# Another order of all engines' steps in a fused memory attention and MLP kernel, and one add moved from GpSimd to VectorE

## The chip, the cores and the metric

The kernel runs on one core of a Trainium2 chip. The time is device time in microseconds from launch to end; three runs of the kernel before gave a median of 710.39 us (709.92 to 711.08). The profile names the core's engines PE (TensorE, matrix products; its weight loads are shown apart as PEld), DVE (VectorE), ACT (ScalarE), POOL (GpSimd) and SP (SyncE, which here only issues DMA transfers).

## The reference

x is 2048 x 512. It is normalized by rows, and the result xn goes into two branches, which meet in one product:

```
out = x + attention(xn) * silu(relu(xn @ w1) @ w2)

attention: 32 heads of 16 columns, 4 segments of 512 rows
for s in range(4):
    logits = qs @ ks.T / 4 + causal mask         # within the segment
    a_dot  = softmax(logits) @ vs
    pq     = phi(qs)                             # t + 1 for t > 0, else exp(t)
    o      = g * (pq @ M) / (pq @ z + 1e-6) + (1 - g) * a_dot     # g = sigmoid(beta), by head
    M     += phi(ks).T @ vs                      # memory, 16 x 16 for each head
    z     += phi(ks).sum(rows)
attention = o @ wo
```

w1 is 512 x 1792, w2 is 1792 x 512, and wq, wk, wv and wo are 512 x 512. All is float32.

## The kernel before

**Precision by parts.** Operands of the large products are split into a rounded part and a rest (names that end in h and l: wh and wl, xh and xl, hh and hl, oh and ol). A product is three matmuls, h x h, h x l and l x h, summed in PSUM. The split of a weight tile of 128 x 512 is one ACT copy (L409, wh) and one POOL subtraction (L410, wl) for each of 176 tiles.

**Halves of the array.** Most products run with 64 rows of the array at a time. `lanes` (L743 and L751) pairs the lower half of a chain's next product with the upper half of an earlier one, so that two streams share PE. A step of three such pairs takes about 0.68 us and is the unit of filler work: the projections to q, k and v, the two MLP products (`w1chain`, `w2chains`) and the output product of all segments but the last.

**A chain of the MLP.** `w1chain` for a block f of 128 hidden columns is four steps on one PSUM bank. Then ACT writes hh (relu, L783), and DVE writes hl (L784), which is the bank's last reader and so sets it free.

**A unit of attention** is 4 heads of one segment, 32 units in all. q and k of two units come from one projection (`projout`, L973 and L974 split it, L977 and L978 write it to DRAM, `stack` reads it back in the shape that the logits need, L1112). `rowmax` has five steps, k0 to k4, of four small matmuls each (L1138), and DVE reduces every block to row maxima (L1144, tile md; a step's bank is free when its reductions are done). `maxrows` turns the maxima (L1162) and sends them through DRAM into the rows of q (L1164, L1165), so that the five `expo` steps (L1190) give logits less their maximum; ACT takes the exponential (P), POOL zeroes above the diagonal (L1197), and `pv` (L1238) multiplies with v. `numden` reads the memory, `memory` and `memory2` add to it; DVE turns phi(k) for it in 16 small transposes (L1072).

**Constants.** `gates` makes the sigmoid of beta and lays it out for each head group: a DMA of beta, a tanh on ACT (L385), and on DVE a step of nine small instructions, here called picks (L370 to L382), which also reads blk, a mask that POOL builds (L336 to L339).

**The end.** `wlast` is the output product of the last segment: row tiles 0, 1 and 2 of 128 rows and 512 columns, and row tile 3 as two halves of 256 columns. `output` multiplies a tile with the gate branch on DVE (L884), adds the rows of x on POOL (L888, with `onpool`) or on DVE (L886) and issues the store (L890). `outhalf` does the same for the halves of tile 3 (L916, L918, L920).

**What sets the order.** Nothing is scheduled at run time. `emit` describes some 4000 steps in a first order, each for one engine: 1121 for PE, 1051 for DVE, 622 for ACT, 525 for POOL and 695 for SP. `Tape.play` then takes them from that list in the order that the string ORDER gives: each letter is the place, in what is left of the list, of the step to emit next. Each engine runs its own steps in that order, and waits where a step needs a result or a buffer of another engine. The string BANKS gives, for each use of PSUM in the first order, the bank that it gets. Both strings were found by a search outside the kernel; the kernel holds only its result. The numbers of steps below count one engine's steps from 0.

Of the kernel before, what the change touches and what calls it, by code (L numbers as in the profile page):

```python
# [77 lines left out]
ORDER = (  # L78
    "0AzByAxwCEAtAsXEqTppTUnTTTkTXiTWgWiAheSBAfSabbbgaAeCAXXN9DNXMMMALTMLLLOADJAPIiJoAHDPAFGFAFDACOpCMISGABAAAODGILeC"
    "HDbEaV1RKXDWWbWGVODFSWUVZUUUaWZCVVCVUUCeVLcXVOZTUnPSSpmkPWlAeQbAgUMWQabXRMJcaLSZUJKPV9LHKNPQMK1NSAMAIOHHIGIJJIG)"  # L80
    "aKMLHKLHIKIIAI^EKJFHJFLFIjFJKHHIHGJGLHIGGGIGIVHGULGGFOFJMFNLIIKJIJKJVLRVJFHOPLJOMKILFJHHoHFQIkG!pIpjHilL15e30GqI"
    "eJnxwkIcH=Gjal*psJentZlhpZhd-hXkYdF5dospgaZFn6kWc3X3lgadHfdeXjalaaXjZjFUdhadfEbSZSWWfXhXeERbeUaSEVRFnTWbPSjZthSP"
    "QplV2PEiOOzRQvCfWphWZanlRVkzAUVQwNwhTMCeNQoOCvaQmWlYRVoCeRTMQOQaJfCTMQMJLbNCUUCjlnQDjKjKiEnRLyJDjQJbCCOCGonLGUCD"
    "SsPDQDoaiCCMhXEWycPclMtgPNYpYNnzeX0XEbYEaVkpYpZVXDiZfUgcXbVZJCaYXSHZVWrVCUUp?JLRbUkiUUPMINcsUZJQpX2nQC0v+vxPKGUC"
    "6t3gdDJFcnCuNE6DWPCopRTPSxlxUOPXhUOOqAKSDPBKvINhNKBQOPdJNODkNiWHRHTOWRKNJOUETNMERNNKhOdMecRc3MD1aDvYYtYuYVDvUBqu"
    "lCLnolnKmuBPglhkqPyngHmBgslHdcghjmeHAbadabe$qAQDkMclDjrYiVfVDBsTTBpEqRRoXzXWxW0XAzFeLaedWArTaVnWEXLiRAQjnEbUNFAF"
    "ZDVWYbLUHaDKCDBaYTdCWbZGCXVCUXTTCBTDBAUTCJWPTPCbACBAEALKFGegDgHgehqHbiOfHgeEveLJaOWpCaIHXjAWBYIAQvdWtVfAadUUPA2S"
    "cYzdSaFgOtY5Slg4jo0malXhvhjbQffQAggUdEjcfEKgUZYcbeUdbAZsJZQIhOZVCaTCHXAfTcAbbTgUTFeEWpcbQmVaDGiTioThgASmejXiiaIf"
    "XaJdcqZpXojdniQkcUKVuFcTiSWSYmRClTGaETZR^BA,R;AAPTPIWEQTCA#RDMSALB/nCJAHpAkFEAhEvzxI)*ftv$vf@fF/}A1-q[h[4EA+}DB8"
    "5]l[41Dr$<x0cnq9u*zAtB3w1A?7hT7fz*56wTxgBDqtV2wV@wtxpTnsSmDqYnemBlhdXPUfaohaWiWYWfcemdjjPUhnbaflZxkUiPctcgTSdnot"  # L90
    "SnmrZlqZhnndAkzkkhdefcRmcbfjRW?Zc>YhOlhqAjkZfnZNcebTceAMQUysBeVASsLSALPPAIJPMITuNAdQLKA@UK#ASL><<IIrNtqlsqAPom/v"
    "Pm-Hsg7?k7B=huiBspByj5n5JAvbkIuxf5kcacmFjnzehhhjiessagqlHihHhbHeieaAHHiLfbhobkAlWKZchYVdAdXbEkOSVZUf&S^HSd^GRSbO"
    "QJIcaXa{X(ZJPFEV2TGYNHEVQCESANCIORIQLqQMADNHHbB=nLAB*/MJqjOHImfPYhdFBDqCkocZABZZAnWeMkkdKCanAWYbBQhUVWeVQYUaUWTF"
    "BTAafSZbScDcRXVVWRxRAxQRAQQqPv2BPRJrAT4NLA3mIllHKjeIhdHLAwrOuwGIrsqsu4usrZq2ALy0x3AwtwqWxtxrlCt1D6p2qy3DGooGEmwl"
    "FtrpjomnBbYjeA1Z2dgAzKBdZMakBgLOAZROkaBMSVfWFccbFScJSRWJYMkHTVGTfUIGFdGakAaZEjYRfAdeTcRvUSQAXXRKYoTUlDdAhUMfaBL9"
    "HGPGLAXeXYMeRSaPtTzTs+PPAO6DVBy2AQFvAuJMfBsIBvHHBsuGuDltrFrDjhiErAfCwfGupznf0rwfwq4udhe0Ec2egxwfiExtkafrlchBomCk"
    "+AU5Ti5BhfPSeNypgcOhheSf+emeScL5bTLxOz-wfeBdQfMNB3wJAkKIxofitoVhHHTeNHkefAihedYtUbQIVcRGWIdPaGaeZPeBFWKkLZidTZKf"
    "gSZeLXAO^4eahKOiSoONfhkQbiQbTZeTQhfXfPRTcQATZeTYAbWSZOkUXQIXWePVGTOSAPXQVAOQMRPHCNDBbMFAaEDAGGXVDTFhRGRFCPEOEYQp"
    "bpPEDSlCP-jQ9C+gJ8IRy5P*0cZNIy6XxICI5ItKHrpJx0HrQCuxPjtntGrFNueyquerFpOnZARmmkZFNlhfXKPldDddbMfaeYQSSOiQtLJAVTCR"
    "PPCXPUcVUTIYCMHeXHeFGFCTcKTCWATWUVRASFLbaENVFDBOWIDCOBPBAQCGLJKALIINKIIGWDIETDNRDIDKCKaFUYICAGJARTMIYERAPGWTANQP"  # L100
    "VOLMoNVTMHFSQJKOJFKQINAJEAIHOGPPNGgNGhMKkmLjiEDhoiegJlbdncchbklb^iiDkhmdigIZAdhHcdrmGepbmnWcjkCjiSAZ^Sf^SEYdAM{b"
    "WdaQbBTXMXZRAGUHLCQGaBSAEWFJKDCRUAHADEALFCCz0ROCJoCLILCJaFFwlJvMCGJnGCKkAIBfAAIBbWWahHkgZkZBiBFefSdaSBaaqGKWpAPn"
    "hNTjfhDVodYgZmQMZWWabdWMYVAWDbBSKTASoAonPnPSIAqiNTn7HfceA2>LKbAyyabwJ5EMYVG01w1<CyFyV-D8k0uu6Dnjj2HQ5l5Hy4nkxgun"
    "hDqioEeikNjjfkgAzUwgAevddMDqiBdnXZBAXBYfzVXXxtbWeqU#qdQ3Aewk1vfxkwXAeW-ssYaebAZbZVgOzaAdeAccfTRkhfPhfeSNhcOQaMGL"
    "hJMYeKcdaUcLZYZMTkLGKPDIFCPbtTPrQcWQQmEvISjOMqhmOICjCQJrBh^CBoZLYVXZaXIp1YoGXKSXjKUwUTuTXScaSEBXTDkTUFbOTIbbRUEM"
    "OFWQSEbLOQjTZDYCMQVBQLPCXWdXBbPMTGiRWgRKFgeBFUceFbaUaEjYBlKSBJTJPNXMbNCUHISFYSNHHUQEXVNEdUKSaMLQNEOCSQCSGOUGNORM"
    "IZUPXYSLTWRDSQ6kSCUQPCCNcfcFcGFZKpYOFlaUjFFSOEseQsqiriHoSvzHuQjxHjtgECvgMdFdDYkEEsIbgiIfaUccljPjdndemdlViiIUagHe"
    "eIMeBPLNaLdZBYLgUceFCUbZUZUfXXEceTcbNHTaBbNDOaYZQXDWPJDqJLpmJDBQESAgBABTGQBBEOJEELCDDCAARMLLANKDRLSQPNPLPANONMMK"
    "LANBGOIRAKPPHYJMZKbKXGMXRMISUkOLikQjFRMjfeTeFLbNlQZMJKEMweNuhTQIopRn3nRI1EwExOGtX1SQeGdryReptJdOBGnwnrEZForWdNDo"
    "blDFjrClVXqEIhkYhTPXCeVdczVyVCVvRDMRRANRAOOODiLMEICJaMaSPNOMBITLSTRIJQJZPHAQNOGOBEMLIQUIPAORQOQKPAJJKLLJNGQIsLRR"  # L110
    "LobQoSmNAQOcFfRAOaYN1Q0KLVvIvREBOINANnALLAjDiQhMGLGKbKmKiakENfgtELWsVaoYDGlgkrgYWJWmEmDgxDfTxbgWXdkbZnijWSyGWWwG"
    "scVrbiFZmHaWFYbVEnJVTDjSjSSXNOehVoNfXUaUVjAD$fhgTffGUHbRwSCPt7vF3Pwgq0wIOuqoAOrEA?DW=Nl-I-WIMJdWbKJk1AXyCWS6NuUR"
    "s1sTIXALX3VHKAXSxEgMlevjhIshLSfMQwMcItjafCEAcmBcwbKCmJDaRBVmEYNDmcWAjEUDTKeCPgRJDdNONJHQIfPBdPPbBiOhOYMOdNPBbBPZ"
    "REbBQBPSPCDnFMDnPjCkDJBJjCBeD8FGZuDE4XrAMicbxHAeAaBEARAFUIFAKQAKASIIMCDAIBEAMAEDAEBGAJABFFBEAGDAECACBBA")
# [53 lines left out]
def emit(tc, PE, ACT, DVE, POOL, SP, cst, ps, dr, args):  # L168
    x2, wq, wk, wv, wo, beta, w1, w2, out2 = args
    S = Tape()  # L170
# [711 lines left out]
    def output(s, t, po, pk, onpool):  # L882
        gt, gk, xr, xk, rows = GX.pop((s, t))
        dve(512, [pk, gk], [gk], lambda: DVE.scalar_tensor_tensor(gt, po, 0.5, gt, op0=OP.mult, op1=OP.mult), 23.7)  # L884
        if not onpool:
            dve(512, [gk, xk], [gk], lambda: DVE.tensor_tensor(gt, gt, xr, op=OP.add), 10.3)  # L886
        else:
            pool(512, [gk, xk], [gk], lambda: POOL.tensor_tensor(gt, gt, xr, op=OP.add), 4.5)  # L888
# [1 line left out]
        dma([gk], [f"out{s}{t}"], lambda: SP.dma_start(out2[rows, :], gt), 10.1, "put")  # L890
# [710 lines left out]
```

## Time and profile before

| | |
|---|---|
| median of 3 runs | 710.39 us (709.92 to 711.08) |
| the profiled execution | 708.85 us |
| its span, first to last instruction | 707.1 us |
| granted TensorE clock | 0.999 |
| PE busy | 691.2 us, 98% |
| DVE, ACT, POOL busy | 70%, 58%, 63% |

The profile is of one execution. A row of the timeline gives the start and the duration in us, the engine, the line of the kernel, the operation, what it writes and reads, and in brackets the idle time of the engine before it and what ended it; "x3" stands for three instructions in a row. A row of waits gives the sum, the number and the longest.

### The profile page before, as it was taken

To read this page: it belongs to the slowest core of one execution; us is meant where nothing else is said; L and a number is where in the kernel's file an instruction comes from. 1 tells how busy PE (TensorE), PEld (TensorE's weight loads), DVE (VectorE), ACT (ScalarE), POOL (GpSimd) and SP (SyncE) were. 2 spreads that over 40 slices of the span, in tenths; PEclk is the share of its full clock that TensorE was granted. 3 is DMA by queue.
4 is the path that set the end of the run, shared out by engine and by line. 5 is a ranking of instruction groups with operands and counts; after the bars stand their busy time and mean duration, and the time that the engine had idled before them with its cause. 6 is when DMAs were issued, how large, how long until landed. Compare 5 with 4: busy or idle time off the path is not lost.

```text
span 707.1 us, 18584 instructions
## 1 busy us (share of the span) xinstructions
PE 691.2 (98%) x6770; PEld 558.5 (79%) x6770; DVE 498.1 (70%) x1591; ACT 407.4 (58%) x621; POOL 447.9 (63%) x571
## 2 busy tenths in 40 slices
PE   9989999999999999999999999999999999999996
PEld 8978777787777788787888779777778878767885
DVE  4189979679968876688965778775778457566347
ACT  5444665566676674476465583756566455655641
POOL 5451775446565686676467876688466676656576
PEclk9999999999999999999999999999999999999999
DMA  6685556556666758876676567866666786944323
GB/s 200 227 274 168 171 192 202 197 153 213 191 237 203 235 163 262 249 209 183 186 224 195 168 217 243 286 197 187 204 205 198 210 280 204 278 139 157 103 60 135
DMA packets 126452, 141.46 MB, mean 200 GB/s; under 512 B 24905, under 2 KB 70217, under 8 KB 126361
## 3 DMA queue, kind: packets, MB, share of 16 engines
...
q8 instruction: 54, 0.88, 0.6%
...
q10 hardware_dynamic: 208, 0.20, 0.1%
...
## 4 chain that ended last, share of the span: by engine, by line
PE 78%; DVE 11%; POOL 3%; ACT 3%; issue 2%; DMA 1%; SPq 1%; DVEq 0%; ACTq 0%; POOLq 0%
PE ps L743 40%; PE ps L751 12%; PE ps L1238 9%; PE ps L1138 5%; PE pt L1190 5%; DVE none L1144 4%; DVE pkT L1072 3%; POOL wl L410 2%; DVE F L1034 1%; DMA nn<-F 1%; PE pt L1024 1%; ACT pq L1032 1%; PE pt L474 1%; PE ps L699 1%; PE ps L701 1%
## 5 line engine op out<-in xcount | busy, mean ns | idle before, releaser
L410 POOL TENSOR_TENSOR wl<-io,wh 128x512 fp32r<-128x512 f32 x176 | 227.6, 1303 | 116.2 <-ACT wh L409 98.4
L1144 DVE CUSTOM_DVE_ANT_0 none<-ps,causal 128x512 bf16<-128x512 f32 (+3 forms) x512 | 249.6, 488 | 61.2 <-PE ps L1138 36.8
L1207 ACT ACTIVATE P<-pt 128x1024 f32<-128x1024 f32 x128 | 131.3, 1026 | 85.8 <-PE pt L1190 65.3
L743 PE MATMUL ps<-xh,wh 64*128 64x512 f32 x352 | 140.9, 400 | 1.0 <-DVE md L1144 0.7
L751 PE MATMUL ps<-xl,wh 64*128 64x512 f32 x352 | 141.4, 402 | 0.0
L751 PE MATMUL ps<-xh,wh 64*128 64x512 f32 x352 | 136.9, 389 | 0.0
L751 PE MATMUL ps<-xh,wl 64*128 64x512 f32 x352 | 136.9, 389 | 0.0
L743 PE MATMUL ps<-xl,wh 64*128 64x512 f32 x352 | 136.7, 388 | 0.0
L743 PE MATMUL ps<-xh,wl 64*128 64x512 f32 x352 | 136.6, 388 | 0.0
L409 ACT ACTIVATE wh<-io 128x512 fp32r<-128x512 f32 x176 | 107.3, 626 | 34.7 <-PE ps L751 23.2
L1197 POOL TENSOR_SCALAR_AFFINE_SELECT P<-P 128x512 f32<-128x512 f32 x128 | 79.8, 639 | 46.7 <-ACT P L1207 33.9
L743 PE MATMUL ps<-wh,hh 64*128 64x512 f32 x224 | 92.0, 411 | 0.4 <-DVE md L1144 0.4
L751 PE MATMUL ps<-wl,hh 64*128 64x512 f32 x224 | 91.3, 408 | 0.0
L751 PE MATMUL ps<-wh,hl 64*128 64x512 f32 x224 | 87.2, 389 | 0.0
L743 PE MATMUL ps<-wl,hh 64*128 64x512 f32 x224 | 87.1, 389 | 0.0
L751 PE MATMUL ps<-wh,hh 64*128 64x512 f32 x224 | 87.0, 389 | 0.0
L743 PE MATMUL ps<-wh,hl 64*128 64x512 f32 x224 | 87.0, 388 | 0.0
L1138 PE MATMUL ps<-ks,qs 64*128 64x512 f32 (+3 forms) x512 | 78.3, 337 | 4.1 <-DVE hl L784 2.7
L1238 PE MATMUL ps<-P,vt 128*17 128x512 f32 (+3 forms) x1024 | 75.1, 434 | 0.1
L743 PEld LDWEIGHTS ps<-xh,wh 64*128 64x128 f32 x352 | 65.0, 185 | 9.6 <-issue 2.9
L743 PEld LDWEIGHTS ps<-xh,wl 64*128 64x128 f32 x352 | 64.8, 184 | 7.4
L1190 PE MATMUL pt<-qs,ks 64*128 64x384 f32 (+3 forms) x512 | 68.3, 311 | 2.2 <-DVE F L1034 1.1
(180 smaller groups left out, 1765.9 us busy)
## 6 DMA issues: line engine op xcount, KB each, us to landing
...
```

The source lines that it names most:

```text
L409: act(512, [rk], [hk], lambda: ACT.activation(h, raw, AF.Copy), 7.0 + nsplit if early else 6.0)
L410: pool(512, [rk, hk], [lk], lambda: POOL.tensor_tensor(l, raw, r32(h), op=OP.subtract), 8.5 + 1.3 * nsplit if early else 25.4)
L474: PE.matmul(pw[:, :128], ident, ident, start=True, stop=True)
L743: i = PE.matmul(m[0], m[2][0][LO], m[2][1][LO], start=m[4], stop=False)
L751: PE.matmul(h[0], h[2][0][HI], h[2][1][HI], start=False, stop=h[5] is not None)
L1072: dve(140, fk, [k], lambda a=a, b=b, i=i: DVE.transpose(pkT[a, :, b], pv[b, i // 4]), 4.0)
L1138: PE.matmul(two[a][0][:, o:o + w], qs[r, p, w - 128:w], ks[r, p, :w], start=True, stop=True)
L1144: dve(w + 40 + TTR, [pk, "causal"], [f"{dk}.{p}{a}{j}"], lambda p=p, j=j, o=o, w=w, a=a, pS=pS: DVE.tensor_tensor_reduce(none[:, :w], pS[: ...
L1190: PE.matmul(pT[:, a, o:o + w], ks[r, p, 128 * i:128 * i + 128], qs[r, p, 128 * i:], start=True, stop=True)
L1197: pool(512, ks, ks, lambda: POOL.affine_select(t, t, pattern=[[0, 4], [1, 128]], compare_op=OP.is_ge, fill=0.0, base=0, channel_multiplier ...
L1207: act(1024, tk, [both[p]], lambda: ACT.activation(P[:, 2 * p:2 * p + 2, :], pT, AF.Exp, scale=0.25), 18.5)
L1238: PE.matmul(pO[32 * b:32 * b + 17, 128 * i:], v, P[:, b, o:o + w], start=i == 0, stop=i == 3)
```

## The change

ORDER and BANKS are replaced. The list of steps, their contents and their buffers other than PSUM banks stay as they are. In `wlast` the argument `onpool` becomes true for row tile 0 alone, where it was true for tiles 0 and 2: tile 2's rows of x are now added on DVE (L886) and not on POOL (L888).

```diff
@@ -62,56 +62,57 @@
 BANKS = (
-    "0123456454253420153452353450551404120452326703670525674146721670311675236751267326733156714140675167234067034673"
...
-    "5673067052761")
+    "0123456454214325014314232155001351341125056754674331672516725675204674206734067206723236713552671467410467012674"
...
+    "4672167456734")
...
 ORDER = (
-    "0AzByAxwCEAtAsXEqTppTUnTTTkTXiTWgWiAheSBAfSabbbgaAeCAXXN9DNXMMMALTMLLLOADJAPIiJoAHDPAFGFAFDACOpCMISGABAAAODGILeC"
-    "HDbEaV1RKXDWWbWGVODFSWUVZUUUaWZCVVCVUUCeVLcXVOZTUnPSSpmkPWlAeQbAgUMWQabXRMJcaLSZUJKPV9LHKNPQMK1NSAMAIOHHIGIJJIG)"
...
-    "s1sTIXALX3VHKAXSxEgMlevjhIshLSfMQwMcItjafCEAcmBcwbKCmJDaRBVmEYNDmcWAjEUDTKeCPgRJDdNONJHQIfPBdPPbBiOhOYMOdNPBbBPZ"
-    "REbBQBPSPCDnFMDnPjCkDJBJjCBeD8FGZuDE4XrAMicbxHAeAaBEARAFUIFAKQAKASIIMCDAIBEAMAEDAEBGAJABFFBEAGDAECACBBA")
+    "0AzAyAxwFABtAsUEqVppVTnUTZkCSXhSWSeSgAiRRdAcdTbTfTWYACaOTYASTDALTQPLLEALL+AIOILEHKHIAGKBAJFbDADYDJHICJERNjGJAgDA"
+    "eBdDCbbgbFaHDYPVGHYFMEVVNNCSMYUKORCTQBPQJOOaRUYSTWMQkMQnPkLNLiJagLXaQJXaAVNcXTTQWXJJPPTPIPJP3OASNLVHNOLJrHLeKAJ)"
...
+    "AABN.jF^AFEkEJBIIBHBHGIAXCIfEBIGOQDHDBFAIIBLGAWCYQXUZWYMVEcLHBBFpNAAocNbHkLHgAGOEGKFCAYCCDZBPBACMBDAJKKNJABHAAHB"
+    "EFEBAAA")
@@ -939,7 +940,7 @@
             if t < 3:
                 yield from project(s, t, *banks[t], us, groups)
                 if groups == one:
-                    output(s, t, *banks[t], t % 2 == 0)
+                    output(s, t, *banks[t], not t)
                 yield M3, False
             else:
```

The search behind the new strings used other durations for the steps, and let a step of PE give free what it reads in parts and not only at its end; none of that is in the kernel.

Read against the list of steps, the new order differs as follows. On PE 227 of 1121 steps keep their place, and a step moves by 2.2 places on average and 21 at most; on DVE 88 of 1051 keep it (6.0 places on average, 63 at most).

*Around picks.* PE's steps 40 to 78 come in the same order in both. On DVE:

- before: hl of f0, the q split (L974), the k split (L974), phi(k) (L991), 16 transposes among which stand the parity step (L364 to L366) and hl of f1 and f2, picks, hl of f3, reductions of unit 0
- after: the parity step, the q split, picks, the k split, phi(k), hl of f0, 15 transposes among which stand hl of f1 and f2, hl of f3, reductions of unit 0; the 16th transpose comes among the later reductions

On ACT the tanh of beta (before behind the relu of f2) comes ahead of the q split, and the exponential of phi(k) (L984) directly behind its relu (before with a weight split between). On POOL blk's last step comes ahead of the weight split of f3 (before behind the splits of three later weights). PE's step 76, `rowmax` k1 of unit 0, writes in both orders one bank that hl of f3 sets free and one that the first reduction sets free.

*Attention against filler.* PE steps from a unit's last `rowmax` step to its first `expo` step, and DVE steps from that `rowmax` step to the unit's last reduction:

| unit | PE steps before | after | DVE steps before | after |
|---|---|---|---|---|
| 3 | 32 | 19 | 8 | 11 |
| 15 | 27 | 21 | 12 | 5 |
| 19 | 32 | 21 | 12 | 5 |
| 30 | 29 | 21 | 11 | 6 |

*The end.* PE's last five steps were the halves of tile 3 (five steps); now they are a last half step of tile 3 twice, and then groups 1, 2 and 3 of tile 1. The last steps of DVE, POOL and SP:

- DVE before: L884 of tiles 0, 2 and 1, L886 of tile 1, L916 of both halves, L918 of both halves
- DVE after: L884 and L886 of tile 2, L916 of the second half, L884 of tile 0, L916 of the first half, L918 of both halves, L884 and L886 of tile 1
- POOL before: L888 of tiles 0 and 2; after: L888 of tile 0
- SP before: stores of tiles 0 and 1, of the first half, of tile 2; after: of tile 2, of the first half, of tiles 0 and 1. The second half is stored from ACT's queue in both.

More of the change, by code (lines that the diff above doesn't have):

```diff
@@ L84 @@
[L84 to L93, printed above, removed]
@@ new lines @@
+    "qlf2AViSQbyRSuZtcpVc^HRDlPW^CTDixRTviRSDtfQqQSDbvRnXUYSqjVfDQTRKPbQPZDwRbLe*!DYPpXD/Tn/vOntGNkGwMii7EhLEf2DKOJJG"
+    "mdhE-FGa8GZVEgFs>GRdDkdmcHP5kqQkDY1z(YfkqYOXcZoGqlDZMmkbYlUOcgUNSbZYZFRQRWVDXdEOVQfQULJDvKT6JNOr2NUoDMHTkGzQitAQ"
+    "JtqROFZSaFjZrwSWrtQoVoFVlNOFzVsRWOTCJSMnLn!LJJNkgN-eUdoQRCRP3PIX=jX0INexNJbJQZLJOoMNmNlCkPSPCeKDE6NubL5sQ2tLCxrt"
+    "LVrsMoykUWvpMjhmLqhDjwCofthmtnfehfmiJdJsDkhePUmQSYQjc1WiEHSTvEcFRKX6QXpCW1PDm2akOT+LRRwxCRCt+SYqHA6BWFtOBTCNRNwD"
+    "RJNtCVECIBFkBP&hRBL@EMiBJOCKIQCBSCQBQPCRJBTQIBNUSKNK2QCOINyJMqPRIOCfojecOqNapRimECqBfnimBxmwh0puyloh7nh+p58F5uMb"
@@ new lines @@
+    "B5uH/CBu3-91wFzWBX6vuF4j3sxxpwDtoTBrmapqTDnnBl2shtLmWMVmBirBWihIngvfklSr3jo1j2j7SizkJhRtiAAzzjwpWtjsJ7Vlqplb32Ov"
+    "jyuxoeR8AFxbj6vw2jPVyAxgIDAEgXXeCEabKeZZBLZPYJLKYECAH#OGVCMLDFoAEpAqnMG3Czm1y{k0p)]mxkFB&u(Kt:E$!rE9[i]{/([pzp]$"
+    "+7B)@,tDA5v2AB4/&978k?$66z>@By3c>Bb2pgA52k2BU0zVqUybkApuoall7xcyaTqmdUepildtTlkrbjyeYmnug5lfpBX3i06i0lYWvkXW1lwW"
+    "dv^Ldo^JtjsV5SqAkh2jhkfrhqCejrZephccQuXjlQcpjkocAcPS6BaTSAa1OYsWANTBSMMSQnSQAKANMTALdMcLWO1OAWuKxt]vAR]1clA$y#p!"
+    "IAz5n03BxmAjkALE+rk1ood5Aidkw0kdylKJuJ2lml1cnzmaxAQjYtiqrXmkjPIihabffDZ^ojh^mgroOeinFXgkB^aZifWWAW^QnXVAMXM^bSgV"
@@ new lines @@
+    "^IXeNEQ!DaGHdDXZaQEVFWPVISYTJCEUAPsSABAP@CSHLPzMH-OnIHMHpbFCC8mqJ5Ckn3LH1HAFrwKApE7bQ6LpcTZ2CWXjjMWtBnYqfwZkYUXr"
+    "ACfoiAm&JgTg@CSC=SCdTQS+f9BRWTRC3RwSRCQBOAONsNSNkAm*86-g6JLAd4N]5{d5R3%vI#A8v4-FvG*8dFZr2kM!y+WAimG-EY6lq1rAooZ1"
+    "xwoTmIlaeIiZDWFQigUAZeVTAWcWAMZSPSBSlbAcRVRODVNAaTAPGXQfVVPcOnTYISjlSVFiHQGSPFajXBlhS^HhXT^EAffxVTcNEmZSPLAhPmJj"
+    "WMDAfhfTKefZiBRXMeNezYPMAVZbYBqD7B<P6B-O3AL/1M0L9Lyy2L!OKKzF/4PwJH1]/2)Ipy+nKA8mCtAljIV/j+i/BFi8AZs{lEgfCBhkuw#k"
+    "CKe?kCgX*BlkjajdAKgWaXUcaXdldqCYNobnbT40c2zkcTPWwXW1dLwyQUcaOTGuyQwhLPLfrrfLH3Gc1kGfGGbceRcN3TYYAFOYQNFaYOqYXBVb"
@@ new lines @@
+    "VTLdNLQJUd^+eULWobUjaJcghZAmiTeciXcggaXZXhWbTXdSaPRZUVXSTQZURSA^NkV^5VAKTAdJTSbPNQ:MOANJILQERMAGHJA=IBHAVHJVTFDE"
+    "TRSReEDOEDsM=D$X=L!D<ZNVD[Q#PP%!&7P#JRa=4?JAa<sItCJ<@Lu7=KtK4qSqK8o7oSS2Co-RyRjlwGseGCI8zi6cdg3nNfElFScjEWWaacaN"
+    "aCt4YTTKJAbdLSDYJAJPKSNlRBLFdARbFAPasRFmAWQJJkCAWRhLHbPBBEZMFBWpGEEQEBeHNDBACJYEZZCMHEUjGSGLEORFEFORECFALKRBL^TJ"
+    "FAQLNQLRgLQRLcEKMCZLQAIBIfTOTRAGFLXGTBMTwCBHQsHPNqOzOo-BwGM8MdE6BRycdeIubcCBLWhyYgWvmHWOAGcAbnaaSUbaSTYV^FeX^TSg"
+    "IVAc^Oc^OPbTKNUXCZWBSWUHARSNPQ[JOJOBXQC!LKQEREUIFsOMDEoCKCDBJpDCKEDrAppADnFsAoFEmDnGCCiiDosoCFrIqAaoBmAkYNIQyggV"
@@ L117 @@
+    "ATq/AtU+XIazZRG*AWP9VPUG8Y7AdXPW2UD9hEy6ilki2jiN-4RVL7DTOMaNM4LX2CbJpaCX0LXWxIVUZSB0SKQUwATGMRrAcxAQEumPArTJSSoD"
+    "AABN.jF^AFEkEJBIIBHBHGIAXCIfEBIGOQDHDBFAIIBLGAWCYQXUZWYMVEcLHBBFpNAAocNbHkLHgAGOEGKFCAYCCDZBPBACMBDAJKKNJABHAAHB"
+    "EFEBAAA")
 RSTEP = (((0, 3, 0),), ((0, 0, 0), (0, 2, 128)), ((0, 1, 0), (1, 1, 256)), ((1, 0, 0), (1, 2, 128)), ((1, 3, 0),))
```

48 lines of the change are left out of this document (19 added, 29 removed).

## Prediction

> **What bounds the kernel now.** I read the head of the page first, then the busy time by stretches of 20 us, then TensorE's own waits.
>
> ```profile
> span 707.1 us, 18584 instructions
> PE 691.2 (98%) x6770; PEld 558.5 (79%) x6770; DVE 498.1 (70%) x1591; ACT 407.4 (58%) x621; POOL 447.9 (63%) x571
> ...
> 20.00:40.00 20.00, 20.00 (x159) 18.75 (x159) 5.57 (x16) 11.50 (x21) 10.45 (x17) 1.00 0.73 233
> 40.00:60.00 20.00, 16.49 (x144) 14.98 (x142) 18.70 (x62) 5.08 (x9) 7.82 (x11) 1.00 0.57 180
> 60.00:80.00 20.00, 19.50 (x208) 16.82 (x206) 18.05 (x68) 12.62 (x19) 10.52 (x14) 1.00 0.74 238
> 80.00:100.00 20.00, 20.00 (x237) 14.73 (x236) 16.91 (x63) 12.29 (x18) 11.01 (x28) 1.00 0.54 177
> ...
> PE ps L1138 <- DVE hl L784: 2.7, 1, 2.7
> PE pt L474 <- POOL epst L267: 1.4, 1, 1.4
> ```
>
> In the stretch rows the numbers after the stretch's length are the busy times of PE, its weight loads, DVE, ACT and POOL, then granted clock, share of the DMA engines and GB/s. PE is busy 98% at full clock: it sets the time, and a change of order, which leaves PE's instructions as they are, can only take away PE's idle time or add to it. That idle time is 707.1 - 691.2 = 15.9 us. 1.4 lie in the opening, and about 5.9 behind the last matmul (shown below). The largest single piece left is one wait of 2.7 us for VectorE's hl, in 40 to 60 us, where DVE is busy 18.70 of 20 while it has only 5.57 of 20 in the stretch before. All other idle time of PE together is 15.9 - 1.4 - 5.9 - 2.7 = 5.9 us.
>
> **The change, first place: the gate constants on VectorE.** What stands before the waiting matmul on DVE, and on PE:
>
> ```profile
> 27.88 0.69 DVE L784 SCALAR_TENSOR_TENSOR hl<-ps,hh 128x512 fp32r<-128x512 f32 x1 [13.07 <-ACT hh L783]
> 30.60 0.69 DVE L974 TENSOR_TENSOR F<-ps,F 128x512 fp32r<-128x512 f32 x1 [2.03 <-ACT F L973]
> 33.81 0.69 DVE L974 TENSOR_TENSOR F<-ps,F 128x512 fp32r<-128x512 f32 x1 [2.52 <-ACT pk L983]
> 36.27 0.69 DVE L991 SCALAR_TENSOR_TENSOR pk<-ps,pk 128x512 f32<-128x512 f32 x1 [1.77 <-ACT pk L984]
> 37.00 2.52 DVE L1072 STREAM_TRANSPOSE pkT<-pk 32x128 f32<-32x128 f32 x8
> 40.43 0.69 DVE L784 SCALAR_TENSOR_TENSOR hl<-ps,hh 128x512 fp32r<-128x512 f32 x1
> 44.03 0.82 DVE L370 TENSOR_SCALAR bt<-bt 128x32 f32<-128x32 f32 x1
> 44.89 1.22 DVE L374 TENSOR_TENSOR mT<-bt,blk 128x32 f32<-128x32 f32 x1
> 46.14 0.18 DVE L376 TENSOR_REDUCE gcol<-mT 64x4 f32<-64x32 f32 x1
> 47.19 0.29 DVE L382 TENSOR_SCALAR gsc<-gsc,par 128x8 f32<-128x8 f32 x1
> 47.39 0.68 DVE L784 SCALAR_TENSOR_TENSOR hl<-ps,hh 128x512 fp32r<-128x512 f32 x1
> 47.99 0.68 DVE L1144 CUSTOM_DVE_ANT_0 none<-ps,causal 128x512 bf16<-128x512 f32 x1
> ...
> 44.50 0.39 PE L743 MATMUL ps<-wh,hh 64*128 64x512 f32 x1
> 44.99 0.39 PE L751 MATMUL ps<-xh,wh 64*128 64x512 f32 x1
> 48.13 0.32 PE L1138 MATMUL ps<-ks,qs 64*128 64x128 f32 x1 [2.74 <-DVE hl L784]
> 48.73 0.55 PE L1138 MATMUL ps<-ks,qs 64*128 64x128 f32 x3 [0.28 <-DVE md L1144]
> ```
>
> The picks step (L370 to L382) holds DVE from 44.03 to 47.48, 3.45 us. Behind it on DVE stands the hl of chain f3 (47.39), which frees the PSUM bank that PE's step 76 (row maximum, L1138) writes. PE has been through since 44.99 + 0.39 = 45.38 and waits 2.74 us.
>
> The new order puts picks between the two L974, where DVE waited 2.52 us for work, and hl of f0 (before at 27.88, in a free place) behind L991. So DVE's work from L991's end at 36.96 to the hl of f3 is now: hl of f0 0.69, 15 transposes at 2.52 / 8 = 0.315, or 4.73, and hl of f1 and f2, 1.38. Sum 6.80: hl of f3 starts at 43.76 in place of 47.39 and ends at 44.45, and the first reduction (L1144, 0.68) ends at 45.13. PE needs both at 45.2 to 45.4, so the wait is gone, and the next one of 0.28 with it at best. DVE comes out 47.39 - 43.76 = 3.6 us earlier, PE 2.74: **term 1 is -2.74 us**.
>
> What picks delays in its new place: it starts at 30.60 + 0.69 = 31.29 and takes 2 us (its nine instructions at the 0.18 to 0.29 of L376 and L382) to 3.45 us (as measured). So the second L974, ready at 33.81, goes at worst at 34.74, 0.93 us late. Queued behind it is the key path: the L978 write, then the stack read for step 73, which PE reached at 43.55.
>
> ```profile
> 34.52 0.32 SPq L978 DMA_DIRECT2D sdk<-F  x1
> 38.17 0.36 SPq L1112 DMA_DIRECT2D ks<-sdk  x1
> ```
>
> From the write to the read that waits for it are 3.65 us. With as much for the read itself the keys were there at 38.17 + 3.65 = 41.8 (an estimate), 1.7 us ahead of 43.55, which covers 0.93. I price this at 0; uncovered it costs 0.93. L991 isn't late: ACT's exponential in front of it has moved ahead of a weight split. Bounds of term 1: 0, if later waits take the gain, and -3.5, all idle time of that stretch (20.00 - 16.49).
>
> **Second place: the end.**
>
> ```profile
> 700.94 0.28 PE L701 MATMUL ps<-wh,ol 128*128 128x256 f32 x1
> 699.49 0.69 DVE L884 SCALAR_TENSOR_TENSOR io<-ps,io 128x512 f32<-128x512 f32 x1
> 700.21 1.50 DVE L886 TENSOR_TENSOR io<-io,bacc 128x512 f32<-128x512 f32 x1
> 701.63 0.41 DVE L916 SCALAR_TENSOR_TENSOR io<-pt,io 128x256 f32<-128x256 f32 x1
> 702.30 1.15 DVE L918 TENSOR_TENSOR io<-io,bacc 128x256 f32<-128x256 f32 x2
> 699.87 2.96 POOL L888 TENSOR_TENSOR io<-io,bacc 128x512 f32<-128x512 f32 x2
> 703.57 0.39 SPq L890 DMA_DIRECT2D out_dram<-io  x1
> ```
>
> PE ends at 701.22. Behind it DVE still has the add of tile 1, two L916 and two L918, and POOL the add of tile 2 until 702.83, whose output is issued last, at 703.57: 2.35 us after PE, and 3.53 before the end of the span. In the new order tile 1 is PE's last, tile 2 is added on DVE (an L886 more there, an L888 less on POOL) several PE steps earlier, and both halves are through before. Behind the last matmul stand only tile 1's L884 (0.69) and L886. I price L886 at 0.69, the row of L884 with the same shape, since POOL's one add left, of tile 0, needs only a PE step that is five places before the last. With three handovers of 0.03 (699.49 + 0.69 = 700.18 to 700.21) that is 0.69 + 0.69 + 0.09 = 1.47 to the issue: **term 2 is 1.47 - 2.35 = -0.88 us**. With the measured 1.50 for L886 it would be -0.07; those are the bounds. The one more issue on SP's queue behind the halves is an old one that changes places.
>
> The row says 1.50 for an add beside POOL's adds and 0.69 for a like instruction elsewhere. The Trainium skill (SBUF — State Buffer, Who interferes with whom) states that a VectorE instruction with two SBUF inputs and a GpSimd instruction that reads SBUF exclude each other, the later one blocking until the earlier ends. By that rule the first L918 would wait for POOL's add of tile 0 and push tile 1's L884 by some 0.2 us, an estimate: term 2 would be -0.7. By the row's 1.50 it is -0.07.
>
> **The rest of the order.** Most steps move by a few places on their engine (on PE by 2.2 on average, on DVE by 6). Row maxima, exponentials and memory reads of many head groups come 2 to 5 us earlier on PE, with filler put behind. No row prices this. At best it takes all the 5.9 us of other idle time; at worst I count as much in new waits, +5.9. I take 0.
>
> **Sum:** 707.1 - 2.74 - 0.88 = 703.48. The profiled execution was 708.85, 1.75 above its span, and the median 710.39 is 1.54 above that execution. So 703.48 + 1.75 + 1.54 = **706.8** for the median.
>
> **The rivals.**
>
> *The gain is taken back in the first segment.* DVE is busy 18.70, 18.05 and 16.91 of 20 from 40 to 100 us. If DVE bounds PE there, PE waits later instead, and only term 2 stays: 709.5. For it: the 18.05. Against: term 1 takes DVE work out of that stretch and not only a wait from PE (3.45 us out, hl of f0 with 0.69 in), and PE idles only 0.50 in 60 to 80.
>
> *Slower: exponentials too early for their row maxima.* One mechanism: between a unit's last row maximum step on PE and its first exponential lie reductions, a transpose on DVE and two small DMAs (L1164, L1165). Unit 19:
>
> ```profile
> 426.04 0.49 PE L1138 MATMUL ps<-ks,qs 64*128 64x512 f32 x2
> 432.85 0.39 SPq L1164 DMA_DIRECT2D mx<-mT  x1
> 436.32 0.58 SPq L1165 DMA_DIRECT2D qs<-mx  x1
> 443.73 0.48 PE L1190 MATMUL pt<-qs,ks 64*128 64x512 f32 x2
> ```
>
> The chain took 436.90 - 426.04 = 10.9 us to the end of the last issue, and the exponential came after 17.7. The new order leaves 32 - 11 = 21 PE steps where there were 32, so about 17.7 x 21 / 32 = 11.6 us at the mean of this row, and with the landing still to come (2 to 3 us, an estimate from the 3.65 above, which has the issue in it) PE would wait about 2 us there. Units 3, 15 and 30 are shortened in the same way (listed with the change), so four times 2 us makes +8, and 706.8 + 8 = 714.8. It outweighs the gain of 3.6 once the four waits exceed 0.9 us each. Against it: for units 15, 19 and 30 the new order has 5 or 6 DVE steps from the last row maximum step to the last reduction, where there were 11 or 12, so the chain is moved up too. With half the waits, 2 of the 4, it would be 710.8.
>
> *More is won.* DVE's peaks are spread better and half or more of the 5.9 us goes too: 706.8 - 4 = 702.8. For it: PE's small waits are nearly all for DVE. Against: they are under 0.5 us each.
>
> *It doesn't do what it says.* picks needs blk from POOL and the tanh from ACT; were one late, DVE would stand with the key path behind it, up to 3 us lost, 709.8. Both stand in the new order ahead of work that PE needs at about the same time (blk's last step ahead of a weight split for chain f3), so this counts little.
>
> **How the numbers follow.** Forecast 0.60; taken back, or picks late, 0.16; slower 0.14; more won 0.10. A measurement of this kernel tells about 0.2% (1.4 us) from no change. Forecast and more won are faster, 0.70; taken back is within, 0.16 with 0.01 less for its upper tail, 0.15; slower 0.15. The forecast's own range is 705.0 to 708.6 (the bounds of terms 1 and 2 mostly). The range for 8 in 10 goes from 702.5 (more won) to 711.8 (0.2% over before, with the smaller of the slower cases).
>
> **What would show it.** Right: no PE wait for hl near 45 us, PE's idle time in 40 to 60 us under 1 us, picks at about 31 us, the second L974 before 34.8, the last issue some 1.5 us behind the last matmul, an L886 near 0.69 there, and PE's idle time in all near 12 us. Wrong: PE waits for md or ACT's P of several tenths repeated over 100 to 650 us, an L1190 waiting for the qs DMA, or an L886 of 1.5 us at the end.

## The result, and the profile after

The new kernel takes 698.89 us (median of 4 runs, 697.13 to 700.62) where the kernel before takes 710.15 beside it (4 runs, 709.43 to 711.08): the ratio is 0.9841, 95% interval 0.9811 to 0.987. The forecast was 706.8 in 702.5 to 711.8. The sign was right; the gain of 11.3 us is three times the 3.6 forecast, and the time lies below the range.

The profiled execution after is the slowest of its four (700.62, span 698.9), that of before lies below its four (708.85, span 707.1), so the two traces differ by 8.2 us only. First the head of the page and the stretches of 20 us, columns as in the prediction:

```profile
span 698.9 us, 18573 instructions
PE 686.7 (98%) x6770; PEld 558.8 (80%) x6770; DVE 497.6 (71%) x1592; ACT 408.2 (58%) x621; POOL 448.5 (64%) x570
...
20.00:40.00 20.00, 20.00 (x156) 17.66 (x156) 8.24 (x28) 13.02 (x23) 11.60 (x18) 1.00 0.81 251
40.00:60.00 20.00, 20.00 (x206) 17.70 (x204) 17.09 (x62) 6.67 (x12) 7.89 (x11) 1.00 0.80 240
60.00:80.00 20.00, 19.96 (x184) 17.59 (x184) 18.34 (x69) 11.30 (x18) 9.96 (x12) 1.00 0.75 241
80.00:100.00 20.00, 20.00 (x240) 15.59 (x230) 17.83 (x63) 13.49 (x18) 14.05 (x32) 1.00 0.59 182
```

PE's idle time is 698.9 - 686.7 = 12.2 us, as forecast (15.9 - 3.6 = 12.3). But PE's busy time has fallen too, from 691.2 to 686.7, with the same 6770 matmuls. By the prediction's reading that could not happen.

The first place, VectorE's line of time in the new kernel (line numbers are one higher than before):

```profile
31.17 0.69 DVE L975 TENSOR_TENSOR F<-ps,F 128x512 fp32r<-128x512 f32 x1 [1.23 <-ACT F L974]
31.78 0.31 DVE L371 TENSOR_SCALAR bt<-bt 128x32 f32<-128x32 f32 x1
32.12 0.19 DVE L375 TENSOR_TENSOR mT<-bt,blk 128x32 f32<-128x32 f32 x1
33.40 0.29 DVE L383 TENSOR_SCALAR gsc<-gsc,par 128x8 f32<-128x8 f32 x1
34.38 0.69 DVE L975 TENSOR_TENSOR F<-ps,F 128x512 fp32r<-128x512 f32 x1 [0.69 <-ACT pk L984]
35.04 0.69 DVE L992 SCALAR_TENSOR_TENSOR pk<-ps,pk 128x512 f32<-128x512 f32 x1
42.62 0.69 DVE L785 SCALAR_TENSOR_TENSOR hl<-ps,hh 128x512 fp32r<-128x512 f32 x1
```

The picks step runs from 31.78 to 33.69 and takes 1.9 us, not 3.45: L371 takes 0.31 (before 0.82) and L375 0.19 (before 1.22). The second L975 starts at 34.38, the hl of f3 at 42.62. PE's longest waits of the new kernel, and the stretch in which the longest lies:

```profile
PE pt L1191 <- DVE F L1035: 2.7, 2, 2.1
PE ps L1139 <- DMA ks<-sdk: 1.6, 2, 0.8
PE pt L475 <- POOL epst L268: 1.4, 1, 1.4
```

```profile
440.00:460.00 20.00, 17.90 (x190) 13.81 (x188) 10.63 (x39) 11.96 (x18) 15.23 (x16) 0.91 0.67 216
```

The wait for hl is gone. There are new ones: for F, behind a ScalarE instruction that waited for a DMA, and for the DMA into ks. The end:

```profile
692.41 1.29 POOL L889 TENSOR_TENSOR io<-io,bacc 128x512 f32<-128x512 f32 x1 [2.02 <-DVE io L885]
692.96 1.37 DVE L919 TENSOR_TENSOR io<-io,bacc 128x256 f32<-128x256 f32 x2 [0.29 <-DMA bacc<-in_A_x_dram]
693.55 0.40 PE L702 MATMUL pt<-wh,ol 128*128 128x512 f32 x1
694.25 0.68 DVE L885 SCALAR_TENSOR_TENSOR io<-pt,io 128x512 f32<-128x512 f32 x1
694.96 0.69 DVE L887 TENSOR_TENSOR io<-io,bacc 128x512 f32<-128x512 f32 x1
694.79 1.22 SPq L891 DMA_DIRECT2D out_dram<-io  x2
```

L887 takes 0.69, as priced. The second of the two L891 is issued at 695.68, 1.73 us behind the end of the last matmul (693.95), where the forecast had 1.47 and the kernel before 2.35. From that end to the end of the span are 4.9 us, before 5.9.

### The profile page after: what moved, and what is told of

Same layout as the page of the kernel before. It is cut to its first block, busy times and chain, and to the rows that moved or that the text cites. A ratio compares the mean times of both kernels' runs of the same rounds, so it can differ in the third digit from the quotient of the medians.

```text
span 698.9 us, 18573 instructions
## 1 busy us (share of the span) xinstructions
PE 686.7 (98%) x6770; PEld 558.8 (80%) x6770; DVE 497.6 (71%) x1592; ACT 408.2 (58%) x621; POOL 448.5 (64%) x570
## 4 chain that ended last, share of the span: by engine, by line
PE 79%; DMA 10%; DVE 3%; POOL 2%; issue 2%; ACT 2%; SPq 1%; DVEq 0%; POOLq 0%; ACTq 0%
PE ps L744 45%; PE ps L752 10%; PE ps L1239 8%; PE ps L1139 6%; PE pt L1191 5%; DMA sdq<-F 2%; DMA ks<-sdk 2%; PE pt L475 1%; DMA nn<-F 1%; DMA io<-in_B_w_dram 1%; DMA dd<-F 1%; PE pt L1025 1%; DMA out_dram<-io 1%; DVE none L1145 1%; DMA sdk<-F 1%
## 5 line engine op out<-in xcount | busy, mean ns | idle before, releaser
L1139 PE MATMUL ps<-ks,qs 64*128 64x512 f32 (+3 forms) x512 | 75.2, 336 | 1.6 <-DMA ks<-sdk 1.6
```

Of the source, the lines that this page charges most:

```text
L1139: PE.matmul(two[a][0][:, o:o + w], qs[r, p, w - 128:w], ks[r, p, :w], start=True, stop=True)
```

## The experiments

Two theories stood at the start. A: the gain is made place by place (first segment, middle, end) and adds up. B: one wait is moved and what comes behind takes it back. The third question came with the page above: what PE's busy time lost. Each kernel was timed beside the kernel before; its median there was 709.6 to 710.4.

| run | median us | ratio to before, 95% | PE busy | span |
|---|---|---|---|---|
| after_again (the new kernel) | 697.56 | 0.9803 to 0.9854 | 685.5 | 697.2 |
| seam_a97 | 705.75 | 0.9922 to 0.9958 | 691.4 | 704.4 |
| seam_b110 | 706.67 | 0.9927 to 0.9969 | 686.5 | 704.7 |
| seam_a409 | 700.41 | 0.9839 to 0.9882 | 688.5 | 700.5 |
| picks_back | 699.57 | 0.9830 to 0.9874 | 686.1 | 696.0 |
| picks_early | 705.87 | 0.9912 to 0.9952 | 690.3 | 704.4 |
| phi_early | 708.84 | 0.9968 to 1.0008 | 690.7 | 706.7 |
| transposes_behind | 710.70 | 0.9988 to 1.0017 | 691.9 | 707.7 |
| before_new_dve | 967.66 | 1.3568 to 1.3649 | 764.6 | 958.0 |
| after_old_dve | 990.30 | 1.3935 to 1.3978 | 773.6 | 985.5 |
| before_new_pe | 965.77 | 1.3569 to 1.3636 | 789.7 | 960.7 |
| after_old_pe | 970.92 | 1.3560 to 1.3678 | 782.6 | 967.7 |
| dma_relief | 697.43 | 0.9807 to 0.9852 | 686.2 | 696.7 |
| late_reductions | 751.26 | 1.0552 to 1.0606 | 708.5 | 748.8 |
| add_on_pool | 698.48 | 0.9820 to 0.9857 | 685.6 | 697.9 |
| end_alone | 710.38 | 0.9994 to 1.0024 | 692.1 | 708.1 |
| old_end | 697.37 | 0.9798 to 0.9849 | 684.8 | 695.5 |

### Where the gain is made: two seams and a third

```diff
 seam_a97:  steps 1..540 played   = new order;  rest = old order, old tile 2
 seam_b110: steps 1..600 played   = old order;  rest = new order, tile 2's add on DVE
 seam_a409: steps 1..2448 played  = new order;  rest = old order, old tile 2
 (BANKS: each take keeps the bank of the order it is played in)
```

> The new order, its banks and nothing else up to the 540th step played (about 97 us), then what is left in the old order with the old banks and the old tile 2 (add on GpSimd). Theory A, gains add up by place: TensorE in the new trace is 3.5 us ahead of the old one at 80 us of its work and 5.0 at 120, so 4.2 at the seam, and the old order keeps that lead: 710.15 - 4.2 = 706.0 us. Rival B, the lead is a shift that the next full stretch of VectorE takes back: 709 to 710, with new TensorE waits for md behind the seam.

> The old order up to its 600th step (about 110 us), then what is left in the new order, the new banks and tile 2's add on VectorE. Theory A: the new trace gains from 4.6 us ahead at the seam to 8.2 at its end, so this one gains 3.6, and up to 5.3 since the executions of the new kernel were 1.7 us apart from their median to the profiled one: 704.9 to 706.5 us, with the old wait of 2.7 us for hl L785 in it. Rival B (the gain hangs on the first 97 us): 709 to 710, no better than the end alone, -0.9.

> The new order up to its 2448th step (about 409 us), then what is left in the old order with the old tile 2. Theory A, gains add up by place: the new trace is 8.1 us ahead there, so 710.1 - 8.1 = 702.0, and TensorE busy near 688. Rival B: half or more is given back behind the seam, 706 or more.

The first 97 us of the new order are worth 4.4 us (710.12 to 705.75), the first 409 are worth 10.0 (710.40 to 700.41), the whole 11.3 to 12.1. Most of a lead is kept behind its seam: in the profiled execution of seam_a97 PE is 3.6 us ahead of before at 97 us and 2.8 at the last matmul, in seam_a409 7.1 at 409 us and 6.3 at the last matmul. So theory B, by which half or more is given back, falls. The parts behind 110 us alone are worth 3.5, less than the 6.9 that 11.3 less 4.4 leaves for them. The line of time of seam_b110 shows one reason, just behind its seam:

```profile
111.38 0.59 SPq L1166 DMA_DIRECT2D qs<-mx  x1
...
113.86 0.50 PE L1191 MATMUL pt<-qs,ks 64*128 64x512 f32 x2 [2.44 <-DMA qs<-mx]
```

This is unit 3's first exponential, and PE waits 2.44 us in front of it for the DMA with the row maxima. The unit's last row maximum step stood at 99.5, at its old place (95.4 in the new kernel), the exponential comes at the new one. With these 2.4 us back, 4.4 + 3.5 + 2.4 = 10.3 of 11.3 are found.

### The first place: the gate constants moved back, moved early in the old order, and the keys' exponential moved alone

```diff
 picks_back (new kernel), DVE:  q split, [-picks,-] k split, phi(k), hl f0, 15 transposes with hl f1, f2, [+picks,+] hl f3
 picks_early (before), DVE:     q split, [+picks,+] k split, phi(k), 16 transposes with hl f1, f2, [-picks,-] hl f3
                       ACT:     tanh of beta ahead of hh of f0;  POOL: pari and blk's last step ahead of two weight splits
 phi_early (before), ACT:       relu of phi(k), [+exponential L984,+] weight split, [-exponential L984-]
```

> The new kernel with only the gate constants (L371 to L383 on VectorE) moved back behind the transposes, just ahead of the hl of chain f3. Theory A (term 1 of the prediction is that step and nothing else): hl of f3 comes 1.9 to 3.4 us later, TensorE waits for it near 45 us, and the time rises by 2 to 3.4 us, to 701 to 702.3 us. Rival C: the new order has slack there from its other moves and takes the step in at either place: 699 to 699.5.

> The kernel before with the gate constants alone moved between the two L974 on VectorE, with the parity step, the tanh on ScalarE and two small GpSimd steps that they need ahead of it. Theory A (term 1): TensorE's wait of 2.7 us near 48 us is gone and stays gone, 710.1 - 2.7 = 707.4. Rival B: the order behind it is as before, VectorE is the limit from 50 to 130 us and takes it back, 709 to 710, with more waits for md.

> The kernel before with one instruction pair changed on ScalarE: the exponential of the keys (L984, 35.6 us in the trace of before) ahead of the weight split that stood before it. With the gate constants in their old late place the new kernel's hl of f3 was still 2.4 us earlier than before's, and L992 1.8 of it. Theory C (that wait had two causes, each worth about as much): L991 comes 1.8 us earlier, the wait for hl falls from 2.7 to about 0.9, 708.3. Theory A (the gate constants alone): nothing, 710.1.

Moved early in the kernel before, with the steps that they need, the gate constants bring 4.5 us, as much as the first 97 us of the new order. But moved back in the new kernel they cost only 0.7 to 2.0 (699.57 against 698.89 and 697.56, with intervals that overlap). That is rival C of the expectation for picks_back: the new order has slack there. In that kernel PE waits for hl and md again, but briefly:

```profile
44.96 0.68 DVE L785 SCALAR_TENSOR_TENSOR hl<-ps,hh 128x512 fp32r<-128x512 f32 x1
...
45.70 0.32 PE L1139 MATMUL ps<-ks,qs 64*128 64x128 f32 x1 [0.37 <-DVE hl L785]
46.31 0.55 PE L1139 MATMUL ps<-ks,qs 64*128 64x128 f32 x3 [0.28 <-DVE md L1145]
```

The hl of f3 starts at 44.96 with the constants in their old late place, 2.4 us earlier than in the kernel before (47.39). L992 stands 1.8 us earlier (34.45 against 36.27), the parity step has left the row of transposes (-0.5), one transpose has gone behind (-0.3), the constants themselves take 2.9 instead of 3.4 (-0.4), and the hl of f0 is in (+0.7): -2.3. So the change removes that wait twice. Most of the 1.8 us of L992 is one instruction on ScalarE, a load of a function table, which before stands between the relu of phi(k) (L983) and its exponential (L984):

```profile
34.31 1.28 ACT L984 ACT_TABLE_LOAD   x1
35.60 0.63 ACT L984 ACTIVATE pk<-pk 128x512 f32<-128x512 f32 x1
```

With the tanh ahead, the load comes in front of the tanh, in idle time of ScalarE (at 26.98 in the new kernel, 25.79 in picks_back, 22.95 in picks_early), and the exponential follows without it. So picks_early moved the load as well as the constants. phi_early left it where it was, at 34.13: L991 came at 36.09, 0.2 us earlier and not the 1.8 expected, PE still waits 2.2 for hl, not 0.9, and the gain is within the interval. That run therefore did not make the condition of its theory C, and says nothing against it. The tanh moved alone in the kernel before would tell the load from the constants; no run has it.

### What PE's busy time lost

At one place, before's PE line of time:

```profile
74.16 0.39 PE L743 MATMUL ps<-xh,wl 64*128 64x512 f32 x1
74.39 0.40 PE L1190 MATMUL pt<-qs,ks 64*128 64x256 f32 x4
75.28 0.50 PE L743 MATMUL ps<-xh,wh 64*128 64x512 f32 x1 [0.50 <-DVE md L1144]
75.62 0.40 PE L743 MATMUL ps<-xl,wh 64*128 64x512 f32 x1
```

Matmuls that take 0.39 each start 0.23 apart, two at a time: each is still counted busy while the next ones run. The Trainium skill (TensorE: Matmul & The Clock Gate, Part 2: What happens when you issue a matmul) says the same: the drain of one matmul overlaps the fill of the next. The exponential step of 74.39 is followed after 0.89 us; in the kernel transposes_behind, where nothing is late there, after 0.23. So PE is 0.66 us late, of which 0.50 are counted idle and 0.16 busy, and the next pair follows after 0.34 instead of 0.23. A lateness of up to 0.16 us (0.39 - 0.23) is not seen as idle time at all. Over a long stretch, before and then after:

```profile
100.00:440.00 340.00, 336.99 (x3478) 272.40 (x3478) 266.74 (x862) 205.49 (x314) 222.43 (x284) 1.00 0.68 206
```

```profile
100.00:440.00 340.00, 337.88 (x3532) 270.77 (x3528) 271.91 (x872) 210.81 (x323) 223.97 (x289) 1.00 0.68 210
```

In the same 340 us PE is busy 337 in both, but starts 54 matmuls more. Counted by steps: the 546 PE steps that take 340.0 us there in the kernel before (step 161 to 707) take 335.1 after, and 334.6 in the new kernel run again. Of these 5 us only 0.9 were idle time (3.0 before, 2.1 after); 4.1 came out of time that was counted busy. From both traces one can take, for each PSUM bank, the time from the end of its last reader to the start of the step that writes it next. Of 901 such hand-overs 65 were below 0.15 us before and 36 after; of the row maximum steps, which write two banks, 19 began before their second bank was free, now 8. Whether such lateness really is counted as busy was tried directly:

```diff
 late_reductions (new kernel), in rowmax(), ahead of the first reduction of each step:
+    DVE.tensor_copy(none[:, :384], causal[:, :384])
     DVE.tensor_tensor_reduce(none[:, :w], pS[:, o:o + w], ...)
```

The copied columns are read by nobody.

> The new kernel with one more instruction of about 0.2 to 0.4 us on VectorE (a copy of 384 columns that nobody reads) ahead of the first reduction of each of the 160 row maximum steps: 30 to 60 us more work there, of 698 us with 200 idle. Theory E (late bank hand-overs are hidden under the ends of earlier matmuls): the time rises by 5 us or more, and at least half of the rise is in TensorE's busy time, not in its idle time. Rival K (busy time is work, and lateness shows as idle): busy stays within 1 us of 686.7 and the whole rise is idle. Rival L (VectorE has slack): time within 1.5 us of the new kernel.

The head of that kernel's page, and the group of the added line:

```profile
span 748.8 us, 18739 instructions
PE 708.5 (95%) x6770; PEld 557.4 (74%) x6770; DVE 576.6 (77%) x1752; ACT 408.4 (55%) x621; POOL 449.6 (60%) x570
...
L1147 DVE COPY none<-causal 128x384 bf16<-128x384 bf16 x160 | 81.3, 508 | 3.8
```

The span grows by 748.8 - 697.2 = 51.6 us against the new kernel beside it, PE's busy time by 708.5 - 685.5 = 23.0, its idle time by 28.6. So 45% of the added time is counted busy, a little under the half expected. Rival K (busy is work) falls, and so does rival L: VectorE idles 200 us of 697, and yet 81 us more work there cost 52.

### Can late hand-overs be mended by hand?

```diff
 transposes_behind (before), DVE, at 20 places from 60 to 500 us:
-  transposes L1072 (1 to 5), instruction that frees a bank late
+  instruction that frees a bank late, transposes L1072
```

> The kernel before, its TensorE order untouched: at 20 places from 60 to 500 us where VectorE freed a PSUM bank less than 0.12 us before TensorE wrote it, the 32x128 transposes (L1072) that stood just ahead of the freeing instruction on VectorE go behind it, 39 in all. Theory E (the part of the gain that was in no idle time of TensorE are late bank hand-overs, covered by the ends of the matmuls before): time falls by 3 to 5 us, to 705 to 707, and TensorE's busy time from 691.2 to 688.5 or less, though its instructions and their order are the same. Rival F (the gain is in TensorE's own order): 709.5 to 710.5 and 691 busy.

No gain: 710.7. At several of its places the edit did what it should. Here is PE in that kernel where before waited at 75.28, and a place where before did not wait:

```profile
74.80 0.40 PE L1190 MATMUL pt<-qs,ks 64*128 64x256 f32 x4
75.03 0.39 PE L743 MATMUL ps<-xh,wh 64*128 64x512 f32 x1
...
129.49 0.50 PE L1190 MATMUL pt<-qs,ks 64*128 64x256 f32 x4 [0.54 <-ACT P L1207]
```

The 0.66 us at the first place are gone, and so are several others (0.46 at 176.8, 0.38 at 163.7 and 122.5, by start-to-start times); in their place stand 0.78 at the exponential above, 0.5 at 77.8, 0.4 at 323, and more small ones. What is let past is late next. This does not refute what theory E says a late bank costs; the step from there to a gain by hand is refuted for these 39 moves.

### Which engine's order is it?

```diff
 before_new_dve: DVE's order of the new kernel (3748 of 4274 differing pairs turned), gate constants early; PE, ACT, POOL, SP as before
 after_old_dve:  new kernel, DVE's order of before (3809 of 4305)
 before_new_pe:  before, PE's order of the new kernel (1011 of 1360)
 after_old_pe:   new kernel, PE's order of before (1105 of 1360)
```

> The kernel before with VectorE's order alone taken from the new kernel, as far as the other engines' old orders and the old banks let it: of 4274 pairs of VectorE steps that the two kernels (with the gate constants early, 705.9 us) play in opposite order, 3748 are turned. Theory G (the rest of the gain is VectorE's order, which frees banks in time): well below the 705.9 of the gate constants alone, 700 to 703, TensorE busy near 687. Rival F (TensorE's own order): 705 to 707, busy 690. Theory H (each engine's order fits only the others' of the same search): no better than 705.9 and perhaps worse than before, as the 39 transposes by hand were.

> The new kernel with VectorE's order alone turned back to the old one (3809 of 4305 pairs). Theory G: most of the gain is lost, 707 to 710. Rival F: 700 to 701. Theory H: 710 or more.

> The kernel before with TensorE's order alone taken from the new kernel (1011 of 1360 pairs turned). Theory G: 709 to 711. Rival F: 703 to 706, the wait for hl still in it. Theory H: slower than before.

> The new kernel with TensorE's order alone turned back to the old one (1105 of 1360 pairs). Theory G: 699 to 701. Rival F: 704 to 708. Theory H: 705 or more.

Theory H, far beyond what was expected: PE's order or VectorE's in the other kernel's company costs 36 to 40% over the kernel before. In before_new_pe:

```profile
PE 789.7 (82%) x6770; PEld 609.2 (63%) x6770; DVE 499.8 (52%) x1591; ACT 408.7 (43%) x621; POOL 445.7 (46%) x571
...
PEclk9999879998999998989999799989989999987998
```

DVE's work is the same (499.8 against 498.1 us), PE's same matmuls take 789.7 busy, part of it by a lower clock: 0.926 was granted in the mean. So the gain could not be assigned to one engine's order. These runs don't tell which pairs of moves make it, and each of them turned only 74 to 88% of the pairs and kept its kernel's banks, so a part of the loss can belong to orders that are neither the old nor the new one.

### The new DMA waits

```diff
 dma_relief (new kernel), ACT: L1033 of head groups 6 and 10 ahead of the L1254 in front of it
                          PE:  row maxima k0 of unit 8 four steps back, of unit 23 six steps back
```

> The new kernel unchanged, beside the next three on one chip. If the 2.1 us wait for F near 447 us and the two for ks (0.8 each) belong to the profiled execution alone, they are absent here and the time is 697 to 699; if they belong to the order, TensorE waits again for DMA-fed work in all 2 to 4 us, at the same places though with other lengths.

> The new kernel with four moves: on ScalarE the two L1033 (numerator and denominator of head groups 6 and 10) go ahead of the L1254 that waited there for the DMA out of F (1.83 and 2.08 us), and on TensorE the first row maxima of units 8 and 23, which waited for the DMA into ks, go four and six steps back. Theory I (the new order paid for its earlier attention steps with waits for DMAs): these waits go, 1.0 to 3.5 us less than the new kernel on the same chip, 695.5 to 698. Rival J (what is moved back is late next, as with the 39 transposes): 698.5 to 700.

The row maxima came out three PE steps later for each unit, not four and six. PE's waits in the new kernel, run again:

```profile
PE pt L475 <- POOL epst L268: 1.4, 1, 1.4
PE ps L1139 <- DMA nn<-F: 1.0, 1, 1.0
PE ps L700 <- ACT oh L1337: 1.0, 1, 1.0
PE ps L1139 <- DMA ks<-sdk: 0.9, 1, 0.9
```

The wait of 2.1 us for F belonged to the profiled execution; waits of row maxima for DMAs (ks 1.6 there, ks and nn 1.9 here) come in both, and before has none. With the four moves they are gone, and others come (L1139 and L637 for md, 0.5 each): 697.43 against 697.56. The time lies in theory I's range, but the gain of 1.0 to 3.5 us over the new kernel beside it is not there: it is 0.1. So what rival J says happens, and these waits are no price that these moves take off.

### The end

```diff
 add_on_pool (new kernel): output(s, t, *banks[t], [-not t-]{+t % 2 == 0+})
 end_alone: steps 1..3920 = old order, rest = new order, tile 2's add on DVE
 old_end:   steps 1..3768 = new order, rest = old order, tile 2's add on POOL
```

> The new kernel, its order untouched, with tile 2's input rows added on GpSimd again in place of VectorE. Theory A: the end's 0.9 us come from the order (tile 2 is through long before tile 1), so 698.9 give or take 0.3. Rival D: they come from the engine of the add: 699.8, with the last output store about 2.3 us behind the last matmul as before.

> The old order up to its 3920th step (about 685 us), then what is left in the new order, with tile 2's add on VectorE. Term 2 of the prediction: -0.9, 709.3. If the end is worth nothing by itself: 710.1; the last store's issue lies 1.5 to 2.1 us behind the last matmul by term 2, 2.35 without it.

> The new order up to its 3768th step (about 640 us), then what is left in the old order, the old banks and the old tile 2 on GpSimd: the reverse of end_alone, which came out 0.8 us above before (710.38 against 709.62), with a tail 1.0 us shorter and a last matmul 2 us later. Theory M (the new last stretch costs TensorE, through its new waits for oh and ol, about what its shorter tail saves): the new kernel less 0.8, or the same, 696.8 to 698.0 where the new kernel was 697.6 and 698.9. Term 2 as predicted: 0.9 above the new kernel, 698.5 to 699.8.

The engine of tile 2's add makes no difference (698.48). The new end alone gains nothing (710.38 against 709.62; by the interval between 0.4 us gained and 1.7 lost), and the new kernel loses nothing that shows with the old end (697.37 against 697.56, an interval of 1.8 us to each side). The last rows of end_alone on PE and SP:

```profile
702.85 0.40 PE L701 MATMUL pt<-wh,ol 128*128 128x512 f32 x1
703.61 0.34 SPq L920 DMA_DIRECT2D out_dram<-io  x1
704.05 1.22 SPq L890 DMA_DIRECT2D out_dram<-io  x2
```

From the last matmul's end (703.25) to the end of the span, 708.1, are 4.9 us, 1.0 less than before. But the last matmul comes 2.0 us later than before's 701.22, and these are lost between 685 and 694 us, right behind the seam, partly in waits for wl (0.37) and bacc (0.48). So this run does not price the end by itself. The reverse run does better: by the starts of PE's steps the new kernel is 8.1 us ahead of before at 640 us and 7.3 at the last matmul (run again, 10.7 and 9.0). It loses 0.8 to 1.7 there, with waits for oh (0.2 to 1.0) and ol (0.4) that before has not, and wins 1.0 in the tail. old_end is 11.2 us ahead at 640 us and 11.3 at the last matmul. The traces bear theory M out; the times alone, with their interval of 1.8 us, would not tell it from the 0.9 of term 2.

Of all kernels, old_end and dma_relief are as fast as the new one; none beats it by more than 0.2%.

## Why the prediction was right or wrong

**What bounds it.** PE sets the time: right. The step that failed is the sentence that a change of order "can only take away PE's idle time or add to it", and with it the 5.9 us as the most that the rest of the order could bring. PE's busy time holds lateness: of the time added by late reductions 45% (late_reductions), at 75.28 us 0.16 of 0.66, and from step 161 to 707 4.1 of the 5 us that the new order wins there. The bound had to be taken from the starts of PE's steps. Take for each pair of successive PE steps the time from start to start, less the 30th percentile of all pairs of the same two kinds over both kernels: these sum to about 40 us before and 30 after, and two thirds of the difference lie behind row maximum steps (13.0 before, 6.5 after). It is a rough measure, since the last matmul came only 7.3 us earlier, but it looks where the gain is. That fewer late hand-overs make the gain behind 97 us is argued from these counts; no run took the lateness out by itself.

**Term 1**, -2.74: the mechanism was there, step by step. picks came at 31.78 (said: about 31), took the lower bound of 2 us, the second L975 started at 34.38 (said: before 34.8), hl of f3 at 42.62 (said: 43.76, with L992 at its old time; it came 1.2 us earlier, since the table load of 1.28 us was gone from in front of its exponential), no wait for hl, PE idle in 40 to 60 us 0.00 (said: under 1). Its size was short: picks_early is worth 4.5 us. The term counted the idle time, 2.74 and "0.28 at best"; behind the wait hand-overs were late as well. In the trace of picks_early PE gains 2.95 us on before at the step that had waited, 0.6 at the one behind it and 0.3 a little later, 3.8 in all, and its waits for md fall from 2.1 us to 1.3. And picks is not the only way to this gain in the new kernel, as picks_back shows; L991 was looked at only for being late, not for being early, and the table load in front of it was not seen.

**Term 2**, -0.88: in its own terms, from the last matmul to the last issue, it measured 1.73 - 2.35 = -0.62, with L887 at the 0.69 that was chosen over 1.50. What the sum left out is a delay of tile 1's L885. It starts 0.30 us behind the last matmul, right behind the two L919, of which the first took 1.03 beside POOL's L889 and the second 0.42. In add_on_pool, where POOL's adds ended at 692.60, L885 starts 0.04 behind the last matmul and the last issue comes 1.48 behind it. The rule quoted from the Trainium skill (SBUF — State Buffer, Who interferes with whom) gave a push of some 0.2 us and -0.7, and the trace agrees. The whole tail is 1.0 us shorter; the other 0.4 came behind the last issue, and why stays open. But the end as a whole is worth about nothing, as end_alone and old_end show: the sum took PE's own last stretch as unchanged, and it lost there what the tail won.

**The rest**, 0: this is the term that was mis-sized. The whole gain of 11.3, less 4.4 for the first 97 us and nothing for the end, leaves some 7 us, of which 5.6 were made between 97 and 409 us.

**The rivals.** "Taken back": no, each seam kept most of its lead. "Exponentials too early": the mechanism is real, 2.44 us at unit 3 in seam_b110, but only where a seam parts the row maxima from their exponential. In the new kernel the whole chain moved up, further than the argument against this rival had it: for unit 3 from the last row maximum step to the end of the last DMA's issue 5.7 us (95.4 to 101.1), before 14.6 (99.4 to 114.0). Its smaller brother, row maxima waiting for DMAs, was not on the list; these waits are 1.6 to 1.9 us, though dma_relief won nothing by removing them. "More is won" is what happened, and its price of at most 5.9 was the same wrong bound: 706.8 - 5.9 = 700.9 is still above what was measured. "Wrong" would have been repeated waits of PE for md or P; there were none.
